# Six first steps in whole float32, weights split one block later, and single operations for a job's products

## The chip, the cores and the metric

The kernel runs on one core of a Trainium2 chip. The metric is the device time of one execution in microseconds (us). Three runs of the kernel before took 849.15, 849.0 and 844.51 us, median 849.0 us. The profiled execution took 847.22 us, of which the profile's span, from the first to the last instruction, is 845.4 us; 1.8 us lie around it.

## The reference

Inputs: q, k, v and o_gate of shape (4, 8, 768, 40), two gates of shape (4, 8, 768), and two weight pairs w_in (320 x 2048) and w_out (2048 x 320), given in float64. Everything else is float32.

```python
for t in range(S):                                   # mLSTM, 768 steps, per batch and head
    m_new = maximum(f[t] + m, i[t])
    f_s, i_s = exp(f[t] + m - m_new), exp(i[t] - m_new)
    C = f_s * C + i_s * outer(v[t], k[t]);  n = f_s * n + i_s * k[t]
    y[t] = sigmoid(o[t]) * (C @ q[t]) / maximum(abs(n @ q[t]), 1)
x = y as (3072, 320)                                 # 3072 tokens = 4 batches x 768
h = x @ w_in;  x = (h - tanh(h)) @ w_out             # first layer
h = x @ w_in2; g = where(h >= 1, h, where(h <= -1, 0, (h + 1)**2 / 4)); out = g @ w_out2
```

## The kernel before

**Attention in jobs.** The sequence is cut into 6 chunks of 128 steps. A job is one batch and one chunk, 24 in all, in the order chunk, batch. `gates` (L338) turns the gates of a group of chunks into stabilised factors for all 32 heads at once; `decays` (L376) makes the running products and writes factors to DRAM, from which later jobs load them broadcast over partitions (`fb`, `gb`). A `job` (L404) loads `qkraw` and `nat` (k, v and o in natural order), scans the decay matrix of 8 heads (L453, VectorE), multiplies q and k on TensorE (scores, L465), multiplies by the decays (L471), multiplies the result with v (products, L509), adds what comes from the state `C` (L503), normalises (L519 to L526), transposes (L532) and updates the state (L539 to L556). The four jobs of chunk 0 make their decay matrix from a matmul (L444) in place of a load.

**Two layers in blocks and steps.** Four jobs are 512 tokens, a block; there are 6 blocks. A step is one block with one of 16 slices of 128 of the 2048 hidden columns. `step` (L598) makes the hidden slice, `activate` (L620) the activation, and two steps later `second` (L647) adds the slice to the block's result in PSUM. Layer 1 runs blocks 0 to 5, then layer 2 does. Products keep float32 accuracy by splitting each operand into a rounded part and a remainder: 8 matmuls in `step`, 8 in `second`. The first `WIDE` steps of block 0 use the whole float32 operands instead (`wf`, `xf`): 3 matmuls each, which the profile shows as two instructions per matmul.

**Weights.** A slice comes as 64-bit numbers (`load64`, L291, 704 KB) and is converted by `conv64` (L301): two ScalarE passes (L315) and two VectorE passes (L317, L319). `split_w` (L323) then rounds it on ScalarE (L326) and takes the remainder on VectorE (L330, two instructions). A wide step needs the converted slice only; its split serves blocks 1 to 5.

**Order.** Every operation is given to a list scheduler, `Plan` (L73), with an engine, an assumed duration and a priority (lower first, in units of steps; step i has priority about i). `schedule` picks, engine by engine, among what can start; the engines then run their queues in that order. Loads are issued in the planned order on the SP queue. Buffers with the same tag share slots in the order of their creation. Before the end of step 0 planned TensorE gaps are filled with dummy matmuls (`filler`, L752). What the change touches: `RAW`, where raw slices wait; `JOB0`, `JOBD`, `AHEAD`, the priorities of jobs (a job of a later block begins `AHEAD` steps before its share of the block); `GROUPS`, `GATES`, `DECAYS`; `WIDE`; `W_LATE`, the steps by which the split of a wide slice follows its step; `W_CONV`, the priorities of the first conversions.

Of the kernel before, what the change touches and what calls it, by code (L numbers as in the profile page):

```python
# [36 lines left out]
LAG = 2  # L37
FIRST = BLK[0]

RAW = {0: 0, 1: 1, 2: 2, 3: 4, 4: 5, 5: 12, 6: 13, 7: 14}  # L40

LOAD = [-90, -89, -88, -86]
JOB0, JOBD, JOBS = -30, 4, 1.0
AHEAD, LOADS = 4, 3
GROUPS = [(c, c + 1) for c in range(NC)]
GATES = [-95, -29.5, 4, 20, 36, 52]
DECAYS = [-94, -21, 5, 21, 37, 53]
WIDE = 4  # L50
# [176 lines left out]
def mlstm_moe_moe(ctx: ExitStack, tc: tile.TileContext, ig, fg, qk, q3, nat, w1, w2, cst, out):  # L227
# [29 lines left out]
    def wbuf(f, shape, dtype, name):  # L257
        return P.buf(of(wp), shape, dtype, f"w{f}", name)
# [32 lines left out]
    def load64(layer, f, prio):  # L291

        if layer == 0 and f in RAW:
            t = wbuf(RAW[f], [128, 8 * WC], U8, "w64")
        else:
            t = abuf("w64", [128, 8 * WC], U8, 3)
        raw_w[layer, f] = t
        load(prio, lambda: t[:, 0:8 * WC - 3], lambda: (w1, w2)[layer][f].bitcast(U8)[:, 3:8 * WC],
             704, w=[t], rows=5629)

    def conv64(layer, f, prio):  # L301

        t = raw_w.pop((layer, f))
        if layer == 0 and f < WIDE:

            u = wf[f] = wbuf(8 + f, [128, 768], I32, "wf")
            op("POOL", 300, prio - 1, lambda: nc.gpsimd.memset(u[:, WC:768], 0), [], [(u, "z")])
        else:
            u = abuf("w32", [128, WC], I32, 2)
        b = abuf("cvb", [128, WC], F32, 1)  # L310
        x = lambda: t.t.bitcast(I8).rearrange("p (n e) -> p n e", e=8)[:, :, 4]
        v = lambda: t.t.bitcast(I32).rearrange("p (n e) -> p n e", e=2)[:, :, 0]
        a = lambda: u[:, 0:WC].bitcast(F32)
        for o, y in ((a, 1.0), (lambda: b.t, -1.0)):
# [23 lines left out]
    def gates(g, prio):  # L338
        ca, cb = GROUPS[g]
        n = (cb - ca) * L  # L340
        cols = slice(ca * L, cb * L)
        if g == 0:
            fr, i_sb, m_sb = (wbuf(NF - 1 - i, [128 if i == 0 else B * H, L + 1], F32, "gate0") for i in range(3))
            gr = None
        else:
            fr, i_sb, m_sb, gr = (abuf(t, [B * H, L + 1], F32, 1) for t in ("fr", "ig", "mg", "gr"))
        gt[g] = fr, gr
        ld = prio - 4 if g > 1 else -99
        load(ld, lambda: fr[0:32, 0:n], lambda: fg[:, cols], n / 8, w=[fr], rows=n * 4)
        load(ld, lambda: i_sb[0:32, 0:n], lambda: ig[:, cols], n / 8, w=[i_sb], rows=n * 4, eng="ACT" if g == 0 else "SP")  # L350
        op("DVE", 60, prio, lambda: nc.vector.tensor_copy(m_sb[:, 0:1], carry[:, g:g + 1]), [("carry", g)], [m_sb])
        op("DVE", dve(2 * n), prio, lambda: nc.vector.tensor_tensor_scan(
            out=m_sb[:, 1:n + 1], data0=fr[0:32, 0:n], data1=i_sb[:, 0:n],
            initial=carry[:, g:g + 1], op0=ALU.add, op1=ALU.max), [fr, i_sb, m_sb, ("carry", g)], [m_sb])
        if g + 1 < len(GROUPS):
            op("DVE", 60, prio, lambda: nc.vector.tensor_copy(carry[:, g + 1:g + 2], m_sb[:, n:n + 1]), [m_sb], [("carry", g + 1)])
        for o, d, f in ((fr, 0, ALU.add), (fr, 1, ALU.subtract), (i_sb, 1, ALU.subtract)):
            def part(e, o=o, d=d, f=f):
                z = o[0:32, 0:n]
                e.tensor_tensor(out=z, in0=z, in1=m_sb[:, d:n + d], op=f)  # L360

            vec(prio, n, part, [o, m_sb], [o])
            if d:
                x = op("ACT", act(n), prio, lambda o=o: nc.scalar.activation(o[0:32, 0:n], o[0:32, 0:n], AF.Exp), [o], [o])
                if g < 2:
                    exps.append(x)
        t = bank("h" if g < 2 else "tn", "t_i")
        for c in range(cb - ca):
            op("PE", pe(32), prio, lambda c=c: nc.tensor.transpose(  # L369
                t[:, c * 32:c * 32 + 32], i_sb[:, c * L:(c + 1) * L], ident[:32, :32]), [i_sb, "cs"], [t])  # L370
        op("DVE", dve(32 * (cb - ca)), prio, lambda: nc.vector.tensor_copy(
            isT[:, ca:cb, :], t[:, 0:(cb - ca) * 32].rearrange("p (c h) -> p c h", h=32)), [t], [("isT", g)])
# [3 lines left out]
    def decays(g, prio):  # L376

        ca, cb = GROUPS[g]
        n = (cb - ca) * L
        cols = slice(ca * L, cb * L)  # L380
        fr, gr = gt[g]
        for c in range(cb - ca):
            if ca + c:
                op("DVE", dve(2 * L), prio, lambda c=c: nc.vector.tensor_tensor_scan(
                    out=gr[:, c * L:(c + 1) * L], data0=fr[0:32, c * L:(c + 1) * L], data1=zero, initial=1.0,
                    op0=ALU.mult, op1=ALU.add), [fr, "zero"], [gr])
        op("DVE", 60, prio, lambda: nc.vector.memset(
            fr[0:32, 0:n].rearrange("p (c l) -> p c l", l=L)[:, :, 0:1], 0.0), [fr], [fr])
        if g:
            load(prio, lambda: fr_d[:, cols], lambda: fr[0:32, 0:n], 32 * n * 4 / 1024, [fr], [("fr_d", g)], rows=n * 4)  # L390
            load(prio, lambda: gr_d[:, cols], lambda: gr[:, 0:n], 32 * n * 4 / 1024, [gr], [("gr_d", g)], rows=n * 4)

    def jbank(n, what, name):

# [9 lines left out]
    def job(n, at, ld):  # L404
# [54 lines left out]

        sp = [jbank(n, f"s{u}", "t_s") for u in range(2)]  # L460

        def score(h):
            for u in range(2):
                t = qt[u * 64:u * 64 + D]
                nc.tensor.matmul(sp[u][:, h * L:(h + 1) * L], t[:, 512 + h * L:512 + (h + 1) * L],  # L465
                                 t[:, h * L:(h + 1) * L], start=True, stop=True)

        for h in range(HU):
            op("PE", 2 * pe(L, 128, 2), at(1), lambda h=h: score(h), [(qt, 0), (qt, 1)], [sp[0], sp[1]])
        for u in range(2):  # L470
            op("DVE", dve(512), at(2 + u), lambda p=sp[u], d=dk[u][0]: nc.vector.tensor_tensor(  # L471
                out=d(), in0=p.t, in1=d(), op=ALU.mult), [sp[u], dk[u][1]], [dk[u][1]])
# [33 lines left out]
        def pv(d, h):

            for z in (0, 64):
                nc.tensor.matmul(  # L509
                    p[z:z + 64, h * E1:(h + 1) * E1], d[:, z:z + 64], v3()[:, h * E1:(h + 1) * E1],  # L510
                    start=(c == 0 and h == 0), stop=(h == H - 1), skip_group_check=True)

        for u in range(2):
            for i in range(HU):
                h = u * HU + i
                op("PE", 125, at(4), lambda u=u, i=i, h=h: pv(dk[u][0]()[:, i * L:(i + 1) * L], h), [dk[u][1], V], [p])
        pn = lambda: p[:, 0:H * E1].rearrange("p (h e) -> p h e", e=E1)
        dn = abuf("dn", [128, H], F32, 1)
        op("ACT", 180, at(5), lambda: nc.scalar.activation(dn.t, pn()[:, :, D], AF.Abs), [p], [dn])  # L519
# [41 lines left out]
        k = max(i for i in range(NB) if BLK0[i] <= n)  # L561
        if BLK0[k] == n:
            if k == 0:
                xf[0] = P.buf(of(xp), [128, 3, 512], F32, "x1", "xf", 2)
            x1[0, k] = P.buf(of(xp), [128, 5, 512], F32R, "x1", "x1", 2)
        z = slice((n - BLK0[k]) * L, (n - BLK0[k] + 1) * L)
        if k == 0:
            op("ACT", act(384), at(8), lambda: nc.scalar.copy(
                xf[0][:, :, z], px[:, 0:384].rearrange("p (k t) -> p k t", k=3)), [px], [(xf[0], n)])
            if n == BLK[0] - 1:  # L570
                a = xf[0]
                split_x(x1[0, 0], slice(0, BLK[0] * L), lambda: a[:, 0:2, 0:BLK[0] * L], lambda: a[:, 2, 0:BLK[0] * L],
                        [(a, m) for m in range(BLK[0])], "DVE", WIDE - 3, "x", BLK[0] * L, True)
# [107 lines left out]
    def evac(layer, k, prio):  # L681
# [205 lines left out]
```

## Time and profile before

| | |
|---|---|
| runs | 849.15, 849.0, 844.51 us |
| profiled execution | 847.22 us, span 845.4 us |
| TensorE, VectorE busy | 831.9 us (98%), 562.7 us (67%) |
| ScalarE, GpSimd busy | 417.0 us (49%), 134.1 us (16%) |
| mean granted TensorE clock | 0.998 of full |

TensorE is busy nearly throughout, but the dummy matmuls count as busy too, and a share over the whole span hides its stages. In the slices of the profile VectorE is busy eight or nine tenths up to about 200 us and six tenths or less after 300 us, so the stage to about 200 us has to be read by itself: from the start to step 0 at 40.9 us, then block 0 to about 133 us, then block 1 to about 205 us.

### The profile page before, as it was taken

Reading aid. Unit: us, or ns where it says so; the run is one execution under the profiler, and the core shown is the slowest. Engines: PE = TensorE matmul, PEld = TensorE weight load, DVE = VectorE, ACT = ScalarE, POOL = GpSimd, SP = SyncE. Lnnn points to the kernel's source line nnn. Section 1 sums busy time; section 2 is a strip of 40 time slices with the busy share of each in tenths; the row PEclk is TensorE's granted clock in tenths of the full one; section 3 lists DMA queues with packets and bytes.
Section 4 is the critical chain, followed back from the end, with each engine's and each line's share of the span. In section 5 each row is a group of like instructions: output and inputs, shape, how many; then the busy total and the mean of one; then the engine's idle time right before and its main releaser. Section 6 shows DMA issues by size and latency. Waiting matters only on the chain.

```text
span 845.4 us, 13194 instructions
## 1 busy us (share of the span) xinstructions
PE 831.9 (98%) x5027; PEld 691.4 (82%) x5031; DVE 562.7 (67%) x920; ACT 417.0 (49%) x792; POOL 134.1 (16%) x170
## 2 busy tenths in 40 slices
PE   8999998999999999999999999999999999999997
PEld 6647766787888788878888889999999999999997
DVE  6998998888878756565446675565555655655554
ACT  3877755666665534433345553443443433433432
POOL 3231124322223321121003020020100100100000
PEclk9999999999999999999999999999999999999999
DMA  8974557566765432341145320020010000000000
GB/s 220 349 219 141 180 185 246 171 214 223 239 196 171 120 107 90 84 140 39 37 147 158 103 88 1 1 82 1 16 66 0 32 2 1 32 1 1 32 1 31
DMA packets 56515, 88.02 MB, mean 104 GB/s; under 512 B 4708, under 2 KB 37892, under 8 KB 56452
## 3 DMA queue, kind: packets, MB, share of 16 engines
q1 hardware_dynamic: 56404, 87.17, 32.8%
q8 instruction: 39, 0.64, 0.3%
q14 instruction: 24, 0.20, 0.1%
q10 hardware_dynamic: 48, 0.02, 0.0%
HBM read 72.59 MB, written 14.58 MB: 103 GB/s over the span
## 4 chain that ended last, share of the span: by engine, by line
PE 84%; DMA 0%; issue 0%; DVE 0%; DVEq 0%
PE h L612 39%; PE a L655 32%; PE t_o L655 5%; PE t_n L509 2%; PE t_s L465 2%; PE t_n L503 1%; PE t_c L539 1%; PE t_x L532 1%; DMA fb<-fr_d 0%; DVE C L556 0%; PE t_i L369 0%; DVE ob L700 0%; DVE x L526 0%; DVE d L453 0%; DVEq L453 0%
## 5 line engine op out<-in xcount | busy, mean ns | idle before, releaser
L612 PE MATMUL h<-x,w 128*128 128x512 f32 x1504 | 388.9, 397 | 1.9 <-ACT w L326 1.5
L612 PEld LDWEIGHTS h<-x,w 128*128 128x128 f32 x1504 | 275.1, 188 | 57.2 <-ACT w L326 2.8
L643 DVE TENSOR_TENSOR gl<-g,gh 128x512 fp32r<-128x512 f32 x188 | 134.1, 713 | 94.6 <-ACT gh L642 93.5
L642 ACT CAST gh<-g 128x512 fp32r<-128x512 f32 x188 | 116.6, 620 | 117.9 <-DVE g L639 72.8
L655 PE MATMUL a<-gh,w 128*128 128x512 f32 x460 | 150.8, 395 | 0.3 <-ACT gh L642 0.3
L637 ACT ACTIVATE g<-g,half 128x512 f32<-128x512 f32 x96 | 69.4, 723 | 121.1 <-DVE g L635 121.1
L655 PE MATMUL a<-w,gh 128*128 128x320 f32 x576 | 127.7, 308 | 0.0
L639 DVE TENSOR_TENSOR g<-h,g 128x512 f32<-128x512 f32 x96 | 66.3, 691 | 75.5 <-ACT g L637 75.5
L655 PE MATMUL a<-gl,w 128*128 128x512 f32 x276 | 107.1, 393 | 0.0
L655 PEld LDWEIGHTS a<-w,gh 128*128 128x128 f32 x576 | 100.2, 188 | 7.3
L630 ACT ACTIVATE g<-h 128x512 f32<-128x512 f32 x92 | 54.9, 597 | 92.7 <-PE h L612 92.5
L655 PEld LDWEIGHTS a<-gh,w 128*128 128x128 f32 x460 | 85.2, 188 | 18.2 <-ACT gh L642 0.8
L631 DVE TENSOR_TENSOR g<-h,g 128x512 f32<-128x512 f32 x92 | 63.2, 687 | 54.9 <-ACT g L630 54.1
L655 PE MATMUL a<-w,gl 128*128 128x320 f32 x288 | 88.9, 309 | 0.0
L635 DVE TENSOR_SCALAR g<-h 128x512 f32<-128x512 f32 x96 | 66.2, 690 | 8.0 <-PE h L612 8.0
L655 PEld LDWEIGHTS a<-gl,w 128*128 128x128 f32 x276 | 51.6, 188 | 11.1 <-DVE gl L643 0.2
L655 PEld LDWEIGHTS a<-w,gl 128*128 128x128 f32 x288 | 54.0, 188 | 0.0
L583 POOL TENSOR_TENSOR x<-xl,x 128x1024 fp32r<-128x1024 f32 x6 | 14.5, 2412 | 241.1 <-ACT x L582 241.1
L453 DVE TENSOR_TENSOR_SCAN d<-fb,scan_id 128x512 f32<-128x512 f32 x40 | 49.4, 1239 | 4.1 <-PE t_n L509 3.4
L522 POOL TENSOR_TENSOR nat<-nat,dn 128x320 f32<-128x320 f32 x24 | 29.1, 1213 | 99.3 <-DVE dn L521 96.7
L655 PE MATMUL t_o<-w,gh 128*128 128x320 f32 x192 | 43.9, 309 | 0.0
L471 DVE TENSOR_TENSOR d<-t_s,d 128x512 f32<-128x512 f32 x48 | 31.2, 680 | 10.9 <-PE t_s L465 9.1
(105 smaller groups left out, 825.2 us busy)
## 6 DMA issues: line engine op xcount, KB each, us to landing
w<-in_w_dram SPq DMA_DIRECT2D x32, 703.6 KB
nat<-in_nat_dram SPq DMA_DIRECT2D x24, 484.0 KB
fb<-fr_d SPq DMA_DIRECT2D x40, 256.0 KB
qkraw<-in_qk_dram SPq DMA_DIRECT2D x48, 160.0 KB
w_d<-w SPq DMA_DIRECT2D x16, 352.0 KB
w<-w_d SPq DMA_DIRECT2D x16, 352.0 KB
xr_d<-xo SPq DMA_DIRECT2D x18, 256.0 KB
q<-in_q_dram SPq DMA_DIRECT2D x20, 180.0 KB
```

The costliest lines, as they stand in the source:

```text
L453: op("DVE", dve(1024), p, lambda o=dk[u][0], i=f[u][0]: nc.vector.tensor_tensor_scan(out=o(), data0=i(), data1=scan_id, initial=0.0, op0=A ...
L471: op("DVE", dve(512), at(2 + u), lambda p=sp[u], d=dk[u][0]: nc.vector.tensor_tensor(out=d(), in0=p.t, in1=d(), op=ALU.mult), [sp[u], dk[u ...
L522: op("POOL", pool(DM), at(5), lambda: nc.gpsimd.tensor_tensor(out=o3().rearrange("p (h e) -> p h e", e=D), in0=o3().rearrange("p (h e) -> ...
L612: op("PE", pe(n), prio, lambda i=i, c=c, s=s: nc.tensor.matmul(p[:, :n], w[:, c:c + 128], x[:, s, :n], start=(i == 0), stop=(i == 7)), [(w ...
L630: op("ACT", act(n), prio + 0.5 - FFN, lambda: nc.scalar.activation(t[:, :n], p[:, :n], AF.Tanh), [p], [t])
L631: op("DVE", dve(n), prio + 0.5 - FFN, lambda: nc.vector.tensor_tensor(out=t[:, :n], in0=p[:, :n], in1=t[:, :n], op=ALU.subtract), [p, t], [t])
L635: op("DVE", dve(n), prio + 0.5 - FFN, lambda: nc.vector.tensor_scalar(t[:, :n], p[:, :n], -1.0, 1.0, op0=ALU.max, op1=ALU.min), [p], [t])
L637: op("ACT", act(n, 1), prio + 0.5 - FFN, lambda: nc.scalar.activation(t[:, :n], t[:, :n], AF.Square, bias=half[:, 0:1], scale=0.5), [t, "h ...
L639: op("DVE", dve(n), prio + 0.5 - FFN, lambda: nc.vector.tensor_tensor(out=t[:, :n], in0=p[:, :n], in1=t[:, :n], op=ALU.max), [p, t], [t])
L642: op("ACT", act(n), prio + 1 - FFN, lambda: nc.scalar.copy(gh[:, :n], t[:, :n]), [t], [gh])
L643: low = lambda e: e.tensor_tensor(out=gl[:, :n], in0=t[:, :n], in1=gh[:, :n].bitcast(F32), op=ALU.subtract)
L655: mm = lambda o, a, b, start, stop, r, cost: op("PE", cost, prio, lambda: nc.tensor.matmul(o(), a(), b(), start=start, stop=stop), r[0], r[1])
```

## The change

Six steps instead of four use whole float32, so slices 4 and 5 are not split for block 0. The splits of wide slices follow their step by 15 in place of 3 steps, so they move from block 0 to block 1. The conversions of slices 0 to 6 get priorities -14 to -1 in place of -24 to -1, behind more of the first jobs' work. Later jobs begin 6 in place of 4 steps ahead. The scores of a job are one operation in place of four, its products one in place of eight; the matmuls are the same, but nothing can be planned between them. Chunks 0 and 1 share one group of gates, and the factors of chunk 1 are written to DRAM at priority -60 (before: -21). Slots are moved: 15 raw slices now wait in the places of later weights, `w64` has 2 slots (before 3), `xo` 2 (before 3), `cvb` is bfloat16 (before float32), `xf` has its own place.

```diff
-RAW = {0: 0, 1: 1, 2: 2, 3: 4, 4: 5, 5: 12, 6: 13, 7: 14}
+RAW = {f: f + 8 if f < 8 else f + 1 for f in range(NF - 1)}
-AHEAD, LOADS = 4, 3
-GROUPS = [(c, c + 1) for c in range(NC)]
-GATES = [-95, -29.5, 4, 20, 36, 52]
-DECAYS = [-94, -21, 5, 21, 37, 53]
-WIDE = 4
-W_LATE = 3
+AHEAD, LOADS = 6, 3
+GROUPS = [(0, 2)] + [(c, c + 1) for c in range(2, NC)]
+GATES = [-95, 4, 20, 36, 52]
+DECAYS = [-94, 5, 21, 37, 53]
+WIDE = 6
+W_LATE = 15
-W_CONV = [-24, -20, -16, -12, -8, -4, -1]
+W_CONV = [-14, -10, -7, -5, -3, -2, -1]
...
-            t = abuf("w64", [128, 8 * WC], U8, 3)
+            t = abuf("w64", [128, 8 * WC], U8, 2)
...
-            u = wf[f] = wbuf(8 + f, [128, 768], I32, "wf")
+            u = wf[f] = wbuf(f + 1, [128, 768], I32, "wf") if f + 1 < WIDE else abuf("wf", [128, 768], I32, 1)
-        b = abuf("cvb", [128, WC], F32, 1)
+        b = abuf("cvb", [128, WC], BF16, 1)
...
-        if g:
-            load(prio, lambda: fr_d[:, cols], lambda: fr[0:32, 0:n], ...)
-            load(prio, lambda: gr_d[:, cols], lambda: gr[:, 0:n], ...)
+        z = slice(n - L, n)
+        cols = slice(cb * L - L, cb * L)
+        load(max(prio, -60), lambda: fr_d[:, cols], lambda: fr[0:32, z], 16, [fr], [("fr_d", g)], rows=512)
+        load(max(prio, -60), lambda: gr_d[:, cols], lambda: gr[:, z], 16, [gr], [("gr_d", g)], rows=512)
...
-        def score(h):
-            for u in range(2):
...
-        for h in range(HU):
-            op("PE", 2 * pe(L, 128, 2), at(1), lambda h=h: score(h), [(qt, 0), (qt, 1)], [sp[0], sp[1]])
+        def scores():
+            for h in range(HU):
+                for u in range(2):
...
+        op("PE", 200 + 2 * HU * 111, at(1), scores, [(qt, 0), (qt, 1)], [sp[0], sp[1]])
...
-        for u in range(2):
-            for i in range(HU):
-                h = u * HU + i
-                op("PE", 125, at(4), lambda u=u, i=i, h=h: pv(dk[u][0]()[:, i * L:(i + 1) * L], h), [dk[u][1], V], [p])
+        op("PE", 200 + 2 * H * 58, at(4), pv, [dk[0][1], dk[1][1], V], [p])
...
-                xf[0] = P.buf(of(xp), [128, 3, 512], F32, "x1", "xf", 2)
+                xf[0] = abuf("xf", [128, 3, 512], F32, 1)
-                        [(a, m) for m in range(BLK[0])], "DVE", WIDE - 3, "x", BLK[0] * L, True)
+                        [(a, m) for m in range(BLK[0])], "DVE", WIDE - 4, "x", BLK[0] * L, True)
...
-                t = gbuf("xo", [128, 512], F32, 3)
+                t = gbuf("xo", [128, 512], F32, 2)
...
-    gates(1, GATES[1])
-            if i > 1 and a * B == BLK0[k]:
+            if i and a * B == BLK0[k]:
-    decays(1, DECAYS[1])
```

## Rows read from the trace of the kernel before

**Rows 1.** Windows: busy PE, PEld, DVE, ACT, POOL (instructions), clock, DMA, GB/s.

```profile
41.00:131.60 90.60, 84.74 (x489) 57.41 (x490) 82.45 (x140) 63.78 (x125) 22.72 (x35) 1.00 0.59 181
133.50:204.70 71.20, 71.20 (x483) 57.23 (x483) 57.85 (x100) 43.82 (x94) 20.59 (x28) 0.99 0.66 213
```

**Rows 2.** Timeline of PE (start us, us) where block 1 begins, and windows there.

```profile
131.61 0.21 PE L369 MATMUL t_i<-cs,ig 32*128 32x32 f32 x1 [2.81 <-DVE x L526]
...
133.53 2.05 PE L612 MATMUL h<-x,w 128*128 128x512 f32 x4
...
132.00:134.00 2.00, 2.00 (x10) 1.83 (x9) 1.93 (x6) 0.64 (x2) 1.76 (x2) 0.54 0.48 146
134.00:136.00 2.00, 2.00 (x12) 1.16 (x13) 0.99 (x1) 0.92 (x1) 0.24 (x1) 0.61 0.96 360
```

**Rows 3.** Timeline of PE: last products of job 3, then step 0.

```profile
35.16 0.67 PE L509 MATMUL t_n<-nat,d 128*64 128x41 f32 x16
...
40.94 4.95 PE L604 MATMUL h<-xf,wf 128*128 128x512 f32 x10
```

**Rows 4.** Groups by line, VectorE, 20.19 to 40.95 us (busy us, mean ns).

```profile
L319 DVE SCALAR_TENSOR_TENSOR wf<-w,wf 128x704 int32<-128x704 int32 x4 | 4.0, 996 | 0.1
L317 DVE TENSOR_TENSOR wf<-wf,cvb 128x704 int32<-128x704 f32 x4 | 3.5, 872 | 0.2 <-ACT cvb L315 0.2
...
L330 DVE TENSOR_TENSOR w<-wf,w 128x64 fp32r<-128x64 f32 (+1 forms) x4 | 1.9, 507 | 0.0
```

**Rows 5.** Timeline of POOL: v of job 3.

```profile
23.41 0.99 POOL L478 TENSOR_TENSOR nat<-nat,isT 128x328 f32<-128x328 f32 x1 [3.68 <-DMA nat<-in_nat_dram]
```

**Rows 6.** Timeline of PE: a whole-float32 `second`, then one split step.

```profile
50.73 2.84 PE L655 MATMUL a<-gh,wf 128*128 128x512 f32 x6
53.41 1.02 PE L604 MATMUL h<-xf,wf 128*128 128x512 f32 x2
...
82.13 1.98 PE L612 MATMUL h<-x,w 128*128 128x512 f32 x8
...
85.75 1.98 PE L612 MATMUL h<-x,w 128*128 128x512 f32 x8
```

**Rows 7.** Remainders: L643 (page), and a slice's split in VectorE's timeline.

```profile
L643 DVE TENSOR_TENSOR gl<-g,gh 128x512 fp32r<-128x512 f32 x188 | 134.1, 713 | 94.6 <-ACT gh L642 93.5
...
36.52 0.91 DVE L330 TENSOR_TENSOR w<-wf,w 128x64 fp32r<-128x64 f32 x2
```

**Rows 8.** One line's instructions: rounding of a slice (ns min/median/max).

```profile
L326 ACT CAST w<-wf x4: 760/770/783, 26.8 to 50.1; 128x704 fp32r<-128x704 f32 x4
```

**Rows 9.** Part 5 of the page: the later jobs' scans (busy, mean ns).

```profile
L453 DVE TENSOR_TENSOR_SCAN d<-fb,scan_id 128x512 f32<-128x512 f32 x40 | 49.4, 1239 | 4.1 <-PE t_n L509 3.4
```

**Rows 10.** Timeline of PE: products of three jobs (first pair, whole, last pair).

```profile
76.14 0.67 PE L509 MATMUL t_n<-nat,d 128*64 128x41 f32 x16
...
137.94 1.13 PE L509 MATMUL t_n<-nat,d 128*64 128x41 f32 x32
139.00 3.70 PE L612 MATMUL h<-x,w 128*128 128x512 f32 x15
...
363.94 0.67 PE L509 MATMUL t_n<-nat,d 128*64 128x41 f32 x16
364.53 0.50 PE L612 MATMUL h<-x,w 128*128 128x512 f32 x1
364.97 0.67 PE L509 MATMUL t_n<-nat,d 128*64 128x41 f32 x16
365.56 0.73 PE L612 MATMUL h<-x,w 128*128 128x512 f32 x2
```

**Rows 11.** Chain that ended last: a load of `fb`, 256 KB.

```profile
124.65 4.20 DMA fb<-fr_d
```

**Rows 12.** Timeline where block 3 begins: last `xo` copy, third sum.

```profile
295.07 0.58 ACT L691 COPY xo<-a 128x512 f32<-128x512 f32 x1
...
298.63 0.39 PE L655 MATMUL a<-gh,w 128*128 128x512 f32 x1
```

More of the change, by code (lines that the diff above doesn't have):

```diff
@@ L342, in gates @@
         if g == 0:
-            fr, i_sb, m_sb = (wbuf(NF - 1 - i, [128 if i == 0 else B * H, L + 1], F32, "gate0") for i in range(3))
-            gr = None
+            fr, i_sb, m_sb, gr = (wbuf(NF - 1 - i, [128 if i == 0 else B * H, 2 * L + 1], F32, "gate0") for i in range(4))
         else:
@@ L347, in gates @@
         gt[g] = fr, gr
-        ld = prio - 4 if g > 1 else -99
+        ld = prio - 4 if g else -99
         load(ld, lambda: fr[0:32, 0:n], lambda: fg[:, cols], n / 8, w=[fr], rows=n * 4)
@@ L364, in gates @@
                 x = op("ACT", act(n), prio, lambda o=o: nc.scalar.activation(o[0:32, 0:n], o[0:32, 0:n], AF.Exp), [o], [o])
-                if g < 2:
+                if g == 0:
                     exps.append(x)
-        t = bank("h" if g < 2 else "tn", "t_i")
+        t = bank("h" if g == 0 else "tn", "t_i")
         for c in range(cb - ca):
@@ L388, in decays @@
             fr[0:32, 0:n].rearrange("p (c l) -> p c l", l=L)[:, :, 0:1], 0.0), [fr], [fr])
-        if g:
-            load(prio, lambda: fr_d[:, cols], lambda: fr[0:32, 0:n], 32 * n * 4 / 1024, [fr], [("fr_d", g)], rows=n * 4)
-            load(prio, lambda: gr_d[:, cols], lambda: gr[:, 0:n], 32 * n * 4 / 1024, [gr], [("gr_d", g)], rows=n * 4)
+        z = slice(n - L, n)
+        cols = slice(cb * L - L, cb * L)
+        load(max(prio, -60), lambda: fr_d[:, cols], lambda: fr[0:32, z], 16, [fr], [("fr_d", g)], rows=512)
+        load(max(prio, -60), lambda: gr_d[:, cols], lambda: gr[:, z], 16, [gr], [("gr_d", g)], rows=512)
     def jbank(n, what, name):
@@ L460, in job @@
         sp = [jbank(n, f"s{u}", "t_s") for u in range(2)]
-        def score(h):
-            for u in range(2):
-                t = qt[u * 64:u * 64 + D]
-                nc.tensor.matmul(sp[u][:, h * L:(h + 1) * L], t[:, 512 + h * L:512 + (h + 1) * L],
-                                 t[:, h * L:(h + 1) * L], start=True, stop=True)
-        for h in range(HU):
-            op("PE", 2 * pe(L, 128, 2), at(1), lambda h=h: score(h), [(qt, 0), (qt, 1)], [sp[0], sp[1]])
+        def scores():
+            for h in range(HU):
+                for u in range(2):
+                    t = qt[u * 64:u * 64 + D]
+                    nc.tensor.matmul(sp[u][:, h * L:(h + 1) * L], t[:, 512 + h * L:512 + (h + 1) * L],
+                                     t[:, h * L:(h + 1) * L], start=True, stop=True)
+        op("PE", 200 + 2 * HU * 111, at(1), scores, [(qt, 0), (qt, 1)], [sp[0], sp[1]])
         for u in range(2):
@@ L505, in job, with pv @@
                     start=(k == 0), stop=False, skip_group_check=True), [(q, k // 2), C], [p])
[L506 to L511, printed above, removed]
-        for u in range(2):
-            for i in range(HU):
-                h = u * HU + i
-                op("PE", 125, at(4), lambda u=u, i=i, h=h: pv(dk[u][0]()[:, i * L:(i + 1) * L], h), [dk[u][1], V], [p])
+        def pv():
+            for h in range(H):
+                d = dk[h // HU][0]()
+                for z in (0, 64):
+                    t = h % HU * L + z
+                    nc.tensor.matmul(
+                        p[z:z + 64, h * E1:(h + 1) * E1], d[:, t:t + 64], v3()[:, h * E1:(h + 1) * E1],
+                        start=(c == 0 and h == 0), stop=(h == H - 1), skip_group_check=True)
+        op("PE", 200 + 2 * H * 58, at(4), pv, [dk[0][1], dk[1][1], V], [p])
         pn = lambda: p[:, 0:H * E1].rearrange("p (h e) -> p h e", e=E1)
```

## The prediction

> **What bounds the kernel now.** I read it by stages, since one share over the whole span mixes them. First the windows: in block 1 TensorE is busy 71.20 of 71.20 us and VectorE 57.85, 81%; in block 0 TensorE is busy 84.74 of 90.60 us and VectorE 82.45, 91% [rows 1]. So from block 1 on only TensorE's own work counts, while in block 0 a VectorE near its limit makes TensorE wait 5.9 us. The reader should see a second loss at the end of block 0: TensorE waits 2.81 us for a late job, and step 16 begins at 133.53 with the granted clock at 0.54 and then 0.61, near the lower of its two levels (1.2 in place of 2.4 GHz), which costs about 4 x (1 - 0.575) = 1.7 us more [rows 2]. Third, the timeline of TensorE up to step 0: the last products of job 3 end at about 35.7 and step 0 starts at 40.94 [rows 3]. What fills the gaps before it are dummy matmuls, so this stage is paced by the chain of the four first jobs. In the same stage VectorE spends 4.0 + 3.5 us on converting slices 0 to 3, 1.87 a slice, as much on slice 4 and 1.9 on splits: 11.3 us between the jobs' own instructions [rows 4].
>
> **The change, part by part.**
>
> *Conversions behind the jobs.* Before step 0 only slice 0 has to be converted (1.87 us on VectorE), and slice 1 soon after; up to 9.4 us of VectorE work can leave the chain [rows 4]. Lower bound of the gain: 0, if banks and the order of TensorE hold the jobs. Upper bound: v of job 3 lands at 23.41 and takes GpSimd until 24.4 [rows 5]; from the last products' start to step 0 it is 40.94 - 35.16 = 5.8 us [rows 3], so step 0 cannot start before 30.2, a gain of 10.7. I take 6 (step 0 at 35): nearer the 9 us of work that leaves than 0, less slice 1, which must still follow at once. The cover of the other conversions is then the wide steps, which ask for a new slice only every 2.7 to 5.4 us.
>
> *Two more wide steps.* A whole-float32 half of a step takes 53.41 - 50.73 = 2.68 us for its six instructions, so a step 5.36; a split step takes 85.75 - 82.13 = 3.62 [rows 6]. Two steps cost 2 x 1.74 = 3.5 us of TensorE. On VectorE they save two remainders of 0.71 [rows 7].
>
> *Splits moved to block 1.* A split is 0.91 us on VectorE [rows 7] and 0.77 on ScalarE [rows 8]. Six leave the stage up to step 16 (two of them stood before step 0, four in block 0).
>
> *Jobs two steps earlier.* The chain of job 7, on which step 16 waited, gets priority over work of two more steps. For it job 8 puts up to two scans of 1.24 us into block 0 [rows 9]. The loads of each job are issued earlier on SP by the same two steps, behind the same buffers; what is late next is VectorE itself.
>
> *Sum to step 16.* VectorE: 82.45 + 5.7 (11.3 less 3.7 for slices 0 and 1 and 1.9 for two splits) - 3.6 - 1.4 + 2.4 = 85.6 us. At its present share of 91% that is 94.0 us from step 0, so with step 0 at 35 and the 1.9 us between the window's end and step 16 [rows 1, 2], step 16 comes at 130.9. TensorE without waits and at the full clock: 133.5 - 40.9 - 5.9 - 1.7 = 85.0, + 3.5, - 0.7 (below) = 87.8, so step 16 at 122.8. I take the middle, 126.8: VectorE must reach 95%, which seems possible because fewer dependences tie it in the wide steps. Gain 6.7 us against 133.5.
>
> *One operation for a job's products.* In the trace they stand as one stretch of 32 instructions in some jobs and as two of 16 in fourteen (first at 76.14, last at 363.94). The separated pair costs 0.59 + 0.59, and the single matmul between takes 0.44 in place of 0.23 (3.62/16): 1.39 us. The whole stretch costs 139.00 - 137.94 = 1.06 us [rows 10, 6]. So 0.34 us each; two pairs lie in block 0 (0.7, used above), twelve where TensorE never rests: -4.1. Bounds: 0 if the gaps only move to the ends of the stretch, -6 if each end costs as much as each inner gap. The scores run in one stretch in every later job already: 0. What waits for it: the products now need both decay halves, but their second half always did.
>
> A completion signal per operation could cost as well. The whole stretch has eight operations and takes 1.06/32 = 33 ns per instruction of 41 columns [rows 10]; at the 2.68/6/512 = 0.87 ns per column of the wide matmuls [rows 6] the columns alone take 36 ns. So nothing is left for signals inside a stretch, and I take 0. The Trainium skill (TensorE: Matmul & The Clock Gate, section "The cost: per-tile semaphore tail") says that increments on completion serialise at 26.3 ns each; seven per job for products and three for scores would by it, as an estimate, give 24 x 10 x 0.0263 = 6.3 us more. By that rule the sum would be 6 us lower; the trace speaks against it.
>
> *Late splits in block 1.* VectorE rises from 57.85 to 63.4 of 71.2 us (89%), but most of it falls on the first six steps, where each needs its split before its first matmul. 0 if they run in the idle time of late block 0, 16 us if all come just in time (rival below). I take +2.5, nearer 0, since splits may start as soon as the wide step is over.
>
> *Two `xo` slots.* The third copy at a block's end must wait until the first is written out. No row shows such a write; a transfer of equal size took 4.20 us in a crowded stage [rows 11]. 295.07 + 4.20 + 0.58 = 299.85, and the bank is wanted at 298.63 [rows 12]: at most 1.2 us at each of six block ends, 7 in all; at best 0. I take +1: later stages are less crowded.
>
> *Edits I cost at nothing.* Gates of two chunks at once lengthen the first instructions on 32 partitions and drop a second series; both hide behind the wait for v of job 3, on which GpSimd sat 3.68 us [rows 5] (without that cover, 1 us either way). The two factor writes pass the raw slices on SP, with nothing behind them that is due within microseconds. `w64` with two slots: a slice of layer 2 is fetched every four steps, 14 us, against landings of 4 [rows 6, 11]. `cvb` in bfloat16: between 0 and half of 0.87 us on 16 conversions, 7 us of VectorE; 0 taken, because the other operand and the result keep 32 bits.
>
> On that last point no run here shows a mixed pair. The Trainium skill (VectorE: DVE Perf Modes, section "What auto-detection actually checks") gives the doubled rate only if every tensor is 16-bit, which would also leave it at 0.
>
> *Total:* -6.7 - 4.1 + 2.5 + 1 = -7.3 us. Against the profiled execution's own 847.2 us: 839.9. That execution stood 1.8 us below the median of the runs shown, 849.0, whose spread is larger, so I leave it at **840**.
>
> **The rivals.**
>
> *A. As forecast*, 840 (own range 834 to 846).
>
> *B. VectorE takes the head start back.* Its work until step 16 hardly falls (it is 85.6 over the longer stage). At 91% step 16 comes at 130.9, a gain of 2.6: -2.6 - 4.1 + 2.5 + 1 = -3.2, 844. For it: TensorE idled 5.9 us at that share. Against it: wide steps use VectorE less than split ones.
>
> *C. Joining the products saves nothing*, that is, the gaps belong to the instruction kind and are paid at the stretch's ends: -7.3 + 4.8 = -2.5, 845. Against it: [rows 10].
>
> *D. Slower: the splits come just in time.* Place: steps 16 to 21. Each cast of 0.77 is released late, then 0.91 of remainder, behind one more VectorE instruction of 0.7 to 1.2: 2.6 us of TensorE wait, six times, 16 us; with B's stage -2.6 - 4.1 + 16 + 1 = +10.3, 857. It decides if a split starts less than 1.7 us before its step, which needs VectorE to be without idle time from step 10 to step 21. For it: its priority is one step before use. Against it: 81% in block 1 [rows 1].
>
> *E. Completions cost inside a stretch too.* A second stretch costs 1.18 - 1.06 = 0.12 us; if a fifth of that, 0.024, stood at every inner signal, 240 fewer save 5.8: 834. The skill's rule above is of this kind. Against it: 33 ns an instruction [rows 10].
>
> **How the numbers follow.** A 0.47, B 0.24, C 0.13, D 0.08, E 0.05, others 0.03. Predicted time: A's 840. Range 832 to 850: E and B inside, the bounds of the start (4 us either way) too; D is left out. What a measurement of this kernel can tell from no change is about 1%, 8.5 us, so the line is at 840.5, next to the forecast: somewhat over half of A (0.29), E (0.05) and a little of B and C (0.06) are faster, 0.40; slower is most of D, 0.07; within 1% 0.53.
>
> **What would show it.** Right: step 0 near 35; step 16 near 127; no wait over 2 us and no granted clock under 0.9 where block 1 begins; every job's products in one stretch of 32; TensorE's work after step 16 shorter by about 4 us. Wrong: step 0 after 38 (the chain of jobs is not paced by VectorE); waits of steps 16 to 21 for L326 or L330 (D); TensorE waiting for the third `xo` copy at block ends; waits for activations in steps 6 to 15 adding up to more than 6 us (B). The forecast fails altogether if conversions of slices 1 to 5 come late for their own wide steps.

## The result, and the profile after

The changed kernel takes 833.7 us (median of four runs, 833.28 to 835.44), the kernel before 848.02 beside it: ratio 0.9842, 95% interval 0.9808 to 0.9876. That is 14.3 us, twice the forecast 7.3, and inside the range, near its lower end. The two profiled executions (847.22 and 835.44 us, spans 845.4 and 833.5) differ by 11.8; the later one stood above its median. I split the 11.9 us by which the spans differ; the experiments below go by medians. New names of lines: the conversions and splits move by one (L330 is L331 now), L444, L453 and L526 are L445, L454 and L528, the scores L467, the products L514 (before L509), `step` L606 and L614, `second` L657, the remainder L645.

Part 1 of the page after, then TensorE's timeline (start us, us), which answers to [rows 2, 3]:

```profile
PE 825.2 (99%) x5012; PEld 686.3 (82%) x5012; DVE 557.6 (67%) x910; ACT 414.6 (50%) x788; POOL 143.1 (17%) x172
```

```profile
28.92 1.13 PE L514 MATMUL t_n<-nat,d 128*64 128x41 f32 x32
...
36.29 1.13 PE L606 MATMUL h<-xf,wf 128*128 128x512 f32 x2 [0.23 <-ACT xf L570]
...
120.14 0.24 PE L369 MATMUL t_i<-cs,ig 32*128 32x32 f32 x1
...
122.35 1.14 PE L614 MATMUL h<-x,w 128*128 128x512 f32 x3
```

Job 3's products are one stretch, 6.2 us before the last of the old halves. Step 0 starts at 36.29 in place of 40.94. The late job that held TensorE for 2.81 us at L369 holds it no longer, and step 16 starts at 122.35 in place of 133.53. The windows from step 0 to step 16 and from there to the end (columns as in rows 1), before and after:

```profile
40.94:133.53 92.59, 86.72 (x500) 59.20 (x500) 84.37 (x144) 64.62 (x127) 24.02 (x37) 0.99 0.59 180
133.53:845.40 711.87, 706.99 (x4183) 605.94 (x4182) 446.79 (x714) 327.01 (x601) 97.86 (x111) 1.00 0.27 84
```

```profile
36.29:122.35 86.06, 86.06 (x485) 56.00 (x486) 77.73 (x129) 60.36 (x120) 29.37 (x35) 1.00 0.68 202
122.35:833.50 711.15, 704.68 (x4188) 606.11 (x4187) 452.04 (x729) 331.72 (x610) 100.96 (x112) 1.00 0.28 85
```

The reader should see that TensorE idled 5.87 us in block 0 before and never after, and that VectorE's work there fell from 84.37 to 77.73 us, where the prediction let it rise by 3.2 (from 82.45 in the window of [rows 1] to 85.6). The granted clock is 1.00 throughout. The stages gave 4.65 us (start), 6.53 (block 0) and 0.72 (the rest). The border is not quite the same in both: before step 16 the groups by line hold 60 + 36 matmuls of split `second` before, and 47 + 27 after, 22 fewer where two steps fewer account for 16. So six or seven slipped behind the border. In a row each takes 0.23 us of TensorE's time (a split step's 16 take 3.62 [rows 6]; the 0.39 that one lasts overlaps the next), so that is about 1.5 us: on equal work block 0 gave about 5.0 and the rest about 2.2.

VectorE's groups in the same stretch (busy us, mean ns; other groups left out), before and after:

```profile
L453 DVE TENSOR_TENSOR_SCAN d<-fb,scan_id 128x512 f32<-128x512 f32 x11 | 13.5, 1238 | 0.7 <-PE t_n L509 0.5 <-DMA fb<-fr_d 0.2
L330 DVE TENSOR_TENSOR w<-w,w 128x64 fp32r<-128x64 f32 (+1 forms) x24 | 12.6, 565 | 0.5 <-ACT w L326 0.5
L317 DVE TENSOR_TENSOR w<-w,cvb 128x704 int32<-128x704 f32 x12 | 11.3, 945 | 0.1
L319 DVE SCALAR_TENSOR_TENSOR w<-w,w 128x704 int32<-128x704 int32 x12 | 11.2, 932 | 0.2
L643 DVE TENSOR_TENSOR gl<-g,gh 128x512 fp32r<-128x512 f32 x12 | 9.6, 799 | 0.4
...
L330 DVE TENSOR_TENSOR w<-wf,w 128x640 fp32r<-128x640 f32 (+1 forms) x5 | 2.8, 575 | 0.0
```

```profile
L454 DVE TENSOR_TENSOR_SCAN d<-fb,scan_id 128x512 f32<-128x512 f32 x10 | 12.7, 1277 | 0.4 <-PE t_n L514 0.4
L331 DVE TENSOR_TENSOR w<-w,w 128x64 fp32r<-128x64 f32 (+1 forms) x20 | 11.8, 625 | 0.2 <-ACT w L327 0.2
L318 DVE TENSOR_TENSOR w<-w,cvb 128x704 int32<-128x704 f32 x10 | 9.6, 955 | 0.0
L320 DVE SCALAR_TENSOR_TENSOR w<-w,w 128x704 int32<-128x704 int32 x10 | 8.9, 887 | 0.2
L645 DVE TENSOR_TENSOR gl<-g,gh 128x512 fp32r<-128x512 f32 x10 | 7.8, 779 | 0.3 <-ACT gh L644 0.2
...
L318 DVE TENSOR_TENSOR wf<-wf,cvb 128x704 int32<-128x704 f32 x2 | 1.8, 893 | 1.1 <-ACT cvb L316 1.0
L320 DVE SCALAR_TENSOR_TENSOR wf<-w,wf 128x704 int32<-128x704 int32 x2 | 1.8, 891 | 0.1
```

Twelve conversions stood there before and twelve stand there now (22.5 and 22.1 us): only one moved in from the start and one moved out behind. The splits fell from 15.4 to 11.8, the remainders by 1.8, the scans by 0.8.

Behind step 16 the products' group fell by 2.2 us; the list of TensorE's longest waits (us in total, times, longest) holds small new ones for the scores (at 159.8, 248.5 and 268.4 us). The products before, the products after, the waits after:

```profile
L509 PE MATMUL t_n<-nat,d 128*64 128x41 f32 x512 | 20.5, 233 | 0.2 <-issue 0.2
```

```profile
L514 PE MATMUL t_n<-nat,d 128*64 128x41 f32 x512 | 18.3, 232 | 0.2 <-DVE d L473 0.2
```

```profile
PE t_s L467 <- issue: 1.4, 2, 1.0
...
PE t_s L467 <- DVE x L590: 0.9, 1, 0.9
```

### The profile page after: what moved, and what is told of

Its sections match the earlier page's. It is cut to its first block, busy times and chain, and to the rows that moved or that the text cites. A ratio compares the mean times of both kernels' runs of the same rounds, so it can differ in the third digit from the quotient of the medians.

```text
span 833.5 us, 13135 instructions
## 1 busy us (share of the span) xinstructions
PE 825.2 (99%) x5012; PEld 686.3 (82%) x5012; DVE 557.6 (67%) x910; ACT 414.6 (50%) x788; POOL 143.1 (17%) x172
## 4 chain that ended last, share of the span: by engine, by line
PE 95%; DMA 2%; ACT 1%; DVE 1%; issue 1%; POOL 0%; SPq 0%; ACTq 0%; DVEq 0%; POOLq 0%
PE h L614 40%; PE a L657 36%; PE t_o L657 5%; PE t_s L467 3%; PE t_n L514 3%; PE h L606 2%; PE t_n L505 1%; PE t_c L541 1%; PE t_f L445 1%; PE spare L757 1%; PE t_x L534 1%; DMA w<-in_w_dram 1%; DMA nat<-in_nat_dram 1%; DVE wf L318 0%; ACT cvb L316 0%
## 5 line engine op out<-in xcount | busy, mean ns | idle before, releaser
L614 PE MATMUL h<-x,w 128*128 128x512 f32 x1488 | 381.5, 395 | 0.0
L614 PEld LDWEIGHTS h<-x,w 128*128 128x128 f32 x1488 | 272.4, 188 | 54.3 <-issue 1.4
L645 DVE TENSOR_TENSOR gl<-g,gh 128x512 fp32r<-128x512 f32 x186 | 133.1, 716 | 90.1 <-ACT gh L644 89.2
L657 PE MATMUL a<-gh,w 128*128 128x512 f32 x450 | 149.3, 395 | 0.0
L657 PE MATMUL a<-w,gh 128*128 128x320 f32 x576 | 127.6, 308 | 0.0
L657 PEld LDWEIGHTS a<-w,gh 128*128 128x128 f32 x576 | 100.2, 188 | 7.3
L657 PE MATMUL a<-gl,w 128*128 128x512 f32 x270 | 105.9, 393 | 0.0
L657 PEld LDWEIGHTS a<-gh,w 128*128 128x128 f32 x450 | 83.3, 188 | 17.2
L657 PE MATMUL a<-w,gl 128*128 128x320 f32 x288 | 88.8, 309 | 0.0
L657 PEld LDWEIGHTS a<-gl,w 128*128 128x128 f32 x270 | 50.7, 188 | 10.9
L657 PEld LDWEIGHTS a<-w,gl 128*128 128x128 f32 x288 | 54.0, 188 | 0.0
L454 DVE TENSOR_TENSOR_SCAN d<-fb,scan_id 128x512 f32<-128x512 f32 x40 | 50.2, 1260 | 0.4 <-PE t_n L514 0.4
L524 POOL TENSOR_TENSOR nat<-nat,dn 128x320 f32<-128x320 f32 x24 | 31.6, 1317 | 104.0 <-DVE dn L523 98.9
L657 PE MATMUL t_o<-w,gh 128*128 128x320 f32 x192 | 43.9, 309 | 0.0
```

What stands on the lines that cost most here:

```text
L454: op("DVE", dve(1024), p, lambda o=dk[u][0], i=f[u][0]: nc.vector.tensor_tensor_scan(out=o(), data0=i(), data1=scan_id, initial=0.0, op0=A ...
L524: op("POOL", pool(DM), at(5), lambda: nc.gpsimd.tensor_tensor(out=o3().rearrange("p (h e) -> p h e", e=D), in0=o3().rearrange("p (h e) -> ...
L614: op("PE", pe(n), prio, lambda i=i, c=c, s=s: nc.tensor.matmul(p[:, :n], w[:, c:c + 128], x[:, s, :n], start=(i == 0), stop=(i == 7)), [(w ...
L645: low = lambda e: e.tensor_tensor(out=gl[:, :n], in0=t[:, :n], in1=gh[:, :n].bitcast(F32), op=ALU.subtract)
L657: mm = lambda o, a, b, start, stop, r, cost: op("PE", cost, prio, lambda: nc.tensor.matmul(o(), a(), b(), start=start, stop=stop), r[0], r[1])
```

## Experiments

Two questions: which part shortened the start, and which took the waits out of block 0. My theory was that every part relieves the same VectorE; the rival, that each removes a loss of its own. Eleven kernels ran, in three sets, each beside the kernel before (847.24, 847.22 and 845.73 us). Within a set and between the first two I compare medians, with the third set ratios: 0.001 is 0.85 us. Timelines and windows are of one execution each.

### The changed kernel once more

No edit.

> The changed kernel once more, so that the others of this call have it on the same chip. All theories: 833 to 836 us, ratio to the kernel before 0.981 to 0.988; step 0 at 36.3 us, step 16 at 122.4 us, no wait of TensorE between them.

833.72 us, ratio 0.9839 (0.9826 to 0.9852): a gain of 13.6 us. This execution began step 0 at 35.88 and step 16 at 121.89. It is the base of the next five.

### One part undone

```diff
-AHEAD, LOADS = 6, 3          # ahead4
+AHEAD, LOADS = 4, 3
-WIDE = 6                     # wide4; xf split with priority WIDE - 2
+WIDE = 4
-W_LATE = 15                  # late3
+W_LATE = 3
-W_CONV = [-14, -10, -7, -5, -3, -2, -1]        # conv_old
+W_CONV = [-24, -20, -16, -12, -8, -4, -1]
-        op("PE", 200 + 2 * H * 58, at(4), pv, ...)      # parted
+        for u in range(2):
+            for i in range(HU):
+                op("PE", 125, at(4), lambda ...: pv(...), [dk[u][1], V], [p])
```

> The changed kernel with jobs 4 instead of 6 steps ahead. Theory 1 (the wait at the start of block 1 went because job 7 came earlier): a wait of 2 to 3 us before step 16 comes back and with it a window of 2 us with a granted clock under 0.8; step 16 at 125 to 128 us, total 3 to 5 us over the changed kernel. Rival (the wait went because VectorE had less to do in block 0, whatever the lead): step 16 at 121.5 to 123.5 us, total within 1 us of the changed kernel.

835.92 us, ratio 0.9870 (0.9856 to 0.9883), 2.2 us slower than the unchanged one, which lies between the theory and the rival. The old wait comes back at the same instruction, half as long, without the lower clock that the theory put with it, and step 16 starts at 125.63. TensorE's timeline, and a window behind the wait (clock 1.00):

```profile
124.32 0.21 PE L369 MATMUL t_i<-cs,ig 32*128 32x32 f32 x1 [1.52 <-DVE x L528]
...
125.63 1.17 PE L614 MATMUL h<-x,w 128*128 128x512 f32 x4
```

```profile
124.00:126.00 2.00, 1.68 (x12) 1.46 (x13) 2.00 (x6) 1.12 (x4) 1.20 (x3) 1.00 0.78 216
```

> The changed kernel with four instead of six whole-float32 steps (the splits of these four still 15 steps late). Theory 1 (the two more wide steps buy VectorE time that is worth about what TensorE pays for them): TensorE work 3.5 us less up to step 16, but waits of 2 to 5 us for splits and remainders in steps 4 to 8; total within 1.5 us of the changed kernel. Rival (VectorE was no limit any more, the two steps cost TensorE 3.5 us for nothing): step 16 3 to 4 us earlier, total 3 to 4 us under the changed kernel.

834.34 us, ratio 0.9846 (0.9833 to 0.986): 0.6 slower, not told apart from nothing. Step 16 starts at 121.31, 0.6 earlier than with six wide steps, but so does step 0 (35.32): the stretch between them is 85.99 us against 86.01. TensorE's busy time in it falls by 1.5 us, not by 3.5, and waits of 0.2 to 0.4 us take that back.

> The changed kernel with the splits of the six wide slices 3 instead of 15 steps after their step. Theory 1 (VectorE is what block 0 lacks): 5.5 us of VectorE work come back into block 0, TensorE waits 2 to 4 us there for L327, L331 or activations; total 1.5 to 4 us over the changed kernel. Rival (VectorE has room in block 0, a split 3 steps late costs nothing): within 1 us, no new waits.

835.09 us, ratio 0.9858 (0.9841 to 0.9876), 1.4 slower; the intervals overlap. TensorE's timeline shows three waits for the remainder in block 0 (rows between left out):

```profile
105.83 0.50 PE L657 MATMUL a<-gl,w 128*128 128x512 f32 x1 [0.45 <-DVE gl L645]
...
110.32 0.96 PE L657 MATMUL a<-gl,w 128*128 128x512 f32 x3 [0.56 <-DVE gl L645]
...
121.58 0.96 PE L657 MATMUL a<-gl,w 128*128 128x512 f32 x3 [0.23 <-DVE gl L645]
...
124.83 1.13 PE L614 MATMUL h<-x,w 128*128 128x512 f32 x4
```

Step 16 comes 2.9 us later than with late splits, and the stretch from there to the end is 2.8 shorter (832.2 - 124.83 = 707.4 against 832.1 - 121.89 = 710.2). About 0.5 of both are two matmuls that stand on the other side of step 16. VectorE is busy 84.24 of 88.96 us from step 0 to step 16, against 78.23 of 86.01: 6.0 us of work come back, and TensorE idles 1.4. So behind step 16 the late splits cost about 2.3, near the forecast 2.5, and half of it is waits of the scores (1.5 us in the unchanged kernel, 0.3 here). In these two profiles they earn about the same ahead of step 16; by medians they earn 1.4 more than they cost.

> The changed kernel with the old priorities of the first seven conversions (-24 to -1). Theory 1 (conversions stood between the jobs' VectorE work): step 0 at 39 to 41 us in place of 36, total 3 to 5 us over the changed kernel. Rival (the start became shorter by the joined products and scores, the conversions fill gaps anyway): step 0 at 35.5 to 37 us, total within 1 us.

832.83 us, ratio 0.9833 (0.9816 to 0.9851), 0.9 faster by medians and 0.5 by ratios: not told apart. Step 0 starts at 36.96, 1.1 later. So in the changed kernel the conversions' priorities are not what made the start short.

> The changed kernel with eight operations for a job's products, as before (scores stay one). Theory 1 (a pair of stretches costs 0.34 us more than one): some 11 to 14 jobs show two stretches of 16, TensorE's busy time after step 16 rises by 3 to 4 us, total 3 to 5 us over the changed kernel. Rival (the gaps are only moved, or the planner splits nothing in this order): total within 1 us.

835.86 us, ratio 0.9862 (0.9849 to 0.9876), 2.1 slower, short of the theory's 3 to 5. Eleven of the jobs have their products in two halves again. Step 0 starts at 35.27, no later than with joined products; the scores' waits of 1.4 us are absent, so the products themselves probably cost more than the 2.1.

### One or two parts done alone

The same edits put into the kernel before: `pv` as one operation (b_joined), `AHEAD` 6 (b_ahead6), both (b_both).

> The kernel before with one operation for a job's products, nothing else changed. Theory 1: no pair of stretches is left, 14 x 0.34 us less where TensorE never rests, less 2 us of new waits as in the changed kernel: 2 to 5 us faster than the kernel before. Rival (the gain of joining in the changed kernel belongs to its other order): within 1 us of the kernel before. The start stage may move either way by up to 2 us in both.

842.12 us, ratio 0.9946 (0.9929 to 0.9963): 5.1 us gained. Step 0 starts at 37.33, with the old conversions. The wait at block 1 stays, and TensorE's timeline and windows, ahead of the wait and behind it, show what it costs this time. The last line is the same stretch ahead of the wait in the kernel before:

```profile
127.86 0.28 PE L369 MATMUL t_i<-cs,ig 32*128 32x32 f32 x1 [2.74 <-DVE x L526]
...
129.91 1.63 PE L612 MATMUL h<-x,w 128*128 128x512 f32 x3
```

```profile
115.10:125.10 10.00, 9.61 (x82) 7.42 (x81) 8.98 (x18) 5.75 (x13) 1.68 (x5) 1.00 0.54 172
127.86:138.00 10.14, 10.14 (x48) 7.78 (x48) 5.51 (x12) 2.89 (x8) 3.88 (x5) 0.51 0.89 309
```

```profile
118.80:128.80 10.00, 9.93 (x81) 7.58 (x81) 8.84 (x17) 5.05 (x13) 3.10 (x5) 1.00 0.56 164
```

After the wait the granted clock stands at 0.51 for ten microseconds: 10.14 x 0.49 = 5.0 us lost, beside 2.7 for the wait. About 4.0 of these fall behind step 16, where the kernel before loses 1.0. The stretch from step 16 to the end, with the same number of matmuls, is 0.3 shorter all the same (711.59 against 711.87), so at an equal clock joining saves about 3.2 there.

> The kernel before with jobs 6 instead of 4 steps ahead, nothing else changed. Theory 1 (job 7 was late only because its priority was): no wait over 1 us and no granted clock under 0.9 before step 16, 3 to 5 us faster than the kernel before. Rival (VectorE is full in block 0, what job 7 gains other work loses): waits of the same sum for L326, L330 or activations in steps 8 to 15, within 1 us of the kernel before.

842.22 us, ratio 0.9943 (0.9927 to 0.9958): 5.0 us gained. The wait at L369 is gone, the clock stays at 1.00, step 16 starts at 129.22. Thirteen jobs keep their products in halves; waits of 1.7 us for L326 remain. Part of the 5.0 is the clock. Of the eleven executions of the kernel before in this set, two show a mean granted clock of 1.00 and take 844.6 us; nine show 0.995 or 0.996 and take 846.6 to 848.2, median 847.35. Against the two, jobs two steps earlier gain 2.4 us, about the wait; the other 2.6 are about what the lower clock costs the kernel before in most of its executions.

> Kernel before with two parts of the change: joined products and jobs two steps earlier. Each alone saved 5.1 and 5.0 us. Theory 'two separate losses' (cut jobs at the start; the late job at step 16): the savings add, -10.1 us, 837 us, step 0 near 37.3 and step 16 near 125.6. Rival 'one loss shared' (both take away waits of the same overloaded VectorE, and a wait removed at one place appears at the next): less than 7 us saved, 840 us or more, waits for L326 or L330 of 2 us or more in block 0.

836.84 us against 845.73, ratio 0.9891 (0.9874 to 0.9908), 9.2 us of 847.2: the two savings, 5.1 and 5.0, add within the interval. (Four of the seven executions of the kernel before in this set have a clock of 1.00; against the other three, median 847.18, the saving is 10.3.) Step 0 at 37.44 is as expected, step 16 at 126.39 is 0.8 later than the sum. Two separate losses, then, and not one shared. The waits for L326 and L330, 2.1 us, stay as they were with either alone: those belong to VectorE's load. What remains to the full change is 4.4 us.

How joining shortened the start can be read from the timelines of the first jobs. First TensorE in b_ahead6 (products parted, conversions early), then VectorE in b_ahead6, in b_both (joined, early) and in parted (parted, conversions behind):

```profile
13.99 0.67 PE L509 MATMUL t_n<-nat,d 128*64 128x41 f32 x16
14.59 0.49 PE L444 MATMUL t_f<-gate,cs 128*128 128x128 f32 x2
15.01 0.67 PE L509 MATMUL t_n<-nat,d 128*64 128x41 f32 x16
```

```profile
13.69 1.22 DVE L453 TENSOR_TENSOR_SCAN d<-t_f,scan_id 128x512 f32<-128x512 f32 x1
...
16.25 1.17 DVE L453 TENSOR_TENSOR_SCAN d<-t_f,scan_id 128x512 f32<-128x512 f32 x1
...
21.69 0.84 DVE L317 TENSOR_TENSOR wf<-wf,cvb 128x704 int32<-128x704 f32 x1
```

```profile
13.38 2.33 DVE L453 TENSOR_TENSOR_SCAN d<-t_f,scan_id 128x512 f32<-128x512 f32 x2
...
20.20 0.84 DVE L317 TENSOR_TENSOR wf<-wf,cvb 128x704 int32<-128x704 f32 x1
```

```profile
13.35 1.21 DVE L454 TENSOR_TENSOR_SCAN d<-t_f,scan_id 128x512 f32<-128x512 f32 x1
...
15.52 1.17 DVE L454 TENSOR_TENSOR_SCAN d<-t_f,scan_id 128x512 f32<-128x512 f32 x1
...
23.70 2.32 DVE L454 TENSOR_TENSOR_SCAN d<-t_f,scan_id 128x512 f32<-128x512 f32 x2
```

With halves, TensorE multiplies job 0's products before it has broadcast all factors (`t_f`) of job 1, and VectorE's second scan of job 1 starts 16.25 - 13.69 = 2.56 us after the first, in place of right behind it. Joined products can't start so early, all broadcasts come first, and everything behind is 1.5 us earlier at the first conversion and 2.2 at step 0 (39.68 against 37.44); 0.3 of both stand there before the scans (13.69 against 13.38). In the third kernel the scans are parted too, but the jobs go ahead of the conversions, and step 0 comes no later. So the conversions' places may be a second way to the same gain; that is not shown, for the third kernel has other edits too, and none of those was added alone to the kernel before. A further 1.3 us of the start is the execution, not the change: b_ahead6, which has the same plan there, begins step 0 at 39.68, not 40.94, and in the profile of before the scores of job 1 wait for their load:

```profile
12.25 0.71 PE L465 MATMUL t_s<-qkraw 40*128 40x128 f32 x6 [0.85 <-DMA qkraw<-in_qk_dram]
```

### Two parts undone; a longer lead

```diff
-WIDE = 6                     # wide4_late3 (changed kernel)
-W_LATE = 15
+WIDE = 4
+W_LATE = 3
-AHEAD, LOADS = 6, 3          # conv_ahead8 (conv_old, and this)
+AHEAD, LOADS = 8, 3
```

> Changed kernel with four wide steps and splits three steps behind, both as before. Undone singly they cost 0.6 and 1.4 us. Theory 'VectorE's load up to step 16 is what these two relieve, and either is nearly enough': undone together they cost more than their sum of 2.0, some 3 to 5 us, 837 to 839, with waits for L326, L330 or L645 of 2 us or more before step 16. Rival 'they act apart': 2.0 us, 835.7; if the 3.5 us of TensorE that the wide steps cost come back as well, 834 or less.

835.08 us against 845.73, ratio 0.9873 (0.9852 to 0.9894): by ratio 2.9 us slower than the unchanged one, between the theories; the intervals hold both. TensorE's windows, first this kernel, then the unchanged one:

```profile
36.00:60.00 24.00, 23.59 (x106) 11.41 (x107) 19.94 (x30) 17.49 (x33) 5.01 (x12) 1.00 0.93 237
60.00:90.00 30.00, 28.32 (x163) 20.99 (x162) 27.45 (x50) 20.54 (x41) 9.53 (x14) 1.00 0.79 258
90.00:126.00 36.00, 33.68 (x229) 24.95 (x228) 34.60 (x62) 26.49 (x54) 8.41 (x11) 1.00 0.35 109
```

```profile
36.00:60.00 24.00, 24.00 (x109) 11.08 (x109) 22.96 (x31) 16.44 (x34) 10.57 (x14) 1.00 0.90 252
60.00:90.00 30.00, 30.00 (x189) 18.90 (x189) 27.03 (x50) 21.45 (x40) 8.88 (x12) 1.00 0.80 260
90.00:126.00 36.00, 36.00 (x217) 28.77 (x215) 31.92 (x56) 23.68 (x51) 10.58 (x15) 1.00 0.35 104
```

TensorE idles 4.4 us again, 0.4 of it ahead of step 0. VectorE is busy 34.60 of the last 36 us, 96%, against 31.92. But the waits of two microseconds for splits or remainders that the theory named are not there (0.8 in all); the longest, 1.5, has no releaser in the records. This execution, 837.46 us, is also the longest of its four, 2.4 above their median, so part of the 4.4 may be its own. That these two parts keep TensorE fed in block 0 is thus seen in this one profile, with 2.9 us by ratio beside it; through which instruction is not shown.

> Changed kernel with the old priorities of the first conversions (0.9 us faster, not told apart from no effect) and jobs eight steps ahead in place of six. Theory 'no wait is left before step 16, so a longer lead finds nothing': 832.8, within 1 us of the kernel with the old conversions alone. Rival 'the longer lead takes the 2.1 us of waits after step 16': 831. Rival 'two more steps of lead load VectorE in block 0': waits before step 16, 834 or more.

836.26 us against 845.73, ratio 0.9879 (0.986 to 0.9898): by ratio 3.9 us slower than with six steps of lead. So a longer lead is not better here. TensorE waits in block 0 (0.5 and 0.8 us) and three times behind it (0.8 each; shorter waits left out), once for a third `xo` copy, which the changed kernel does not show. TensorE's line, then ScalarE's:

```profile
143.57 0.96 PE L657 MATMUL a<-gh,w 128*128 128x512 f32 x3 [0.80 <-ACT xo L693]
```

```profile
142.12 0.92 ACT L316 ACTIVATE cvb<-w,half 128x704 bf16<-128x704 int8 x1
142.95 0.57 ACT L693 COPY xo<-a 128x512 f32<-128x512 f32 x1
```

No variant is shown to beat the changed kernel; conv_old is level with it within the intervals.

## Why the prediction was right, and where it was not

**The direction and the carriers held, one term failed.** The forecast was -7.3; the spans of the profiles differ by -11.9, the medians by -14.3. By stages, on equal work, the forecast was -5.9 (start), -0.8 (block 0) and -0.6 (the rest); measured were -4.65, about -5.0 and about -2.2.

*Conversions behind the jobs* (-6): step 0 came 4.65 us earlier. The size is near by luck, the reason was not right: four conversions and one split still stand before step 0, and undoing their priorities costs 1.1. From 20 us to step 0 VectorE is busy 14.75 of 16.29 us, and 8.4 of these are that work (4.0 + 3.5 + 0.9): the jobs need 6.3 us of it and wait for other engines meanwhile. Of the 4.65, 1.3 were a late load in the profile I read from, about 2 are what joined products bring to the start (b_both against b_ahead6), and about 1 is the conversions' own.

*Two wide steps* (+3.5): not contradicted. TensorE's stretch from step 0, 86.06 us plus the 1.5 that slipped behind it, is 87.6 where I had 87.8 for TensorE without waits. Alone the price is not shown: wide4, without the two, saves 1.5 of TensorE's busy time.

*Sum to step 16* (126.8, with VectorE at 95%): this step failed. Of the 85.6 us that I gave VectorE there, 5.7 were work pushed in from the start, which never came, and 2.4 two early scans, of which none came either (10 scans in place of 11). At 77.73 of 86.06 us VectorE runs at 90%, its old share, and TensorE alone sets the time; step 16 came at 122.35, by my lower bound of 122.8. So block 0 gave about 5.0 on equal work where I had 0.8. Taking the middle between two engines was the mistake, on a load that I had not asked whether it could stay: in the kernel before VectorE was busy 19.75 us from 20 us to step 0, and 11.3 of these were conversions and splits, so the jobs left room there too.

*Joined products behind step 16* (-4.1): their group fell by 2.2 us, and the group of L612, now L614, from 362.4 to 359.4, of which about 1.0 is the half clock of before [rows 2] and the rest the single matmuls between halves: together 4.2. The size is right, though 23 and not all 24 jobs have one stretch; b_joined gives about 3.2 and parted 2.1 for the same edit.

*Completion signals* (0): the term is right, its premise was not. The prediction counts a signal for each planned operation. In the trace of the kernel before, one or two of a job's 32 product instructions raise a semaphore (41 of 768 in all), and in the changed kernel too (43 of 768). So joining took no signals away, and a stretch of 32 takes 1.13 us in both [rows 10]. The rule of the Trainium skill (TensorE: Matmul & The Clock Gate, section "The cost: per-tile semaphore tail"), 26.3 ns for each such increment, is neither borne out nor contradicted by any run here.

*Late splits in block 1* (+2.5): about 2.3 on equal work between late3 and the unchanged kernel. Five of the six splits do run behind the start of step 16 (VectorE, 127 to 149 us), in the changed kernel with no wait for L327 or L331: rival D's place was right, its price was not. Scores late by 1.0 and 0.9 us were the cost that the list shows.

*`xo`* (+1): TensorE has no such wait in the changed kernel. A copy does wait for a write in some runs, 1.6 us in all in ahead4, but TensorE has no wait with it. The 0.80 in conv_ahead8 is another thing: there the copy stands right behind a conversion on ScalarE and waits for no write. *`cvb` in bfloat16* (0): 893 to 1004 ns for L318 where L317 took 872 to 945 [rows 4], so no gain. The Trainium skill (VectorE: DVE Perf Modes, section "What auto-detection actually checks") has it so for tensors of mixed width; the trace agrees.

*The rivals.* B fell with VectorE's load; C fell with the products' group and with b_joined; D as above; E because the number of signals did not change. E's number, 834, came true by another road, and by luck: block 0 without a single wait.

The half clock was booked too small. I took 1.7 us for it, from the profile of before, and took it all off the stretch ahead of step 16, where 0.7 of it lie (1.93 us at 0.64). In b_joined a wait of nearly the same length brought 5.0, and the executions of the kernel before that have it are 2.0 and 2.8 us longer (third and second set, medians) than those at 1.00. What decides between 1.7, 5.0 and none stays open.

## What to carry to other kernels

Where two engines are both near their limit, work out first whether the work that a change moves really has to move: an engine with idle time in the earlier stage keeps it there. An operation cut in pieces lets a planner put its first piece in front of what another engine waits for; joining the pieces can pay far from where they stand. Parts that each cost little when undone can carry most of the gain, when another covers for them: add them one by one to the kernel before as well.

## What was not expected of the hardware

A TensorE wait of 2.7 to 2.8 us was followed by the lower of the two clock levels: for some 3.4 us in the kernel before (0.54 and 0.61 in the windows of [rows 2], 1.7 us lost) and for some ten in b_joined (0.51 over 10.14 us, 5.0 lost). In the ten microseconds ahead of the wait TensorE had been busy 9.93 us in the one and 9.61 in the other, at 1.00. Behind the wait of 1.52 us in ahead4 the clock stayed at 1.00. Of the kernel before, six of 27 executions beside the experiments show a mean clock of 1.00; they were not profiled. So a wait of that size was worth up to 7.7 us and not 2.7.
